# Kernel tables from two small tables of magnitudes, read-outs of the last rows on VectorE, and a new order

## The chip, the cores and the metric

The kernel runs on one core of one Trainium2 chip. A core has five engines with their own instruction queues: PE (TensorE, matrix products; its weight loads are listed as PEld), DVE (VectorE), ACT (ScalarE), POOL (GpSimd) and SP (SyncE, which here issues transfers). All work on an on-chip memory, SBUF, of 128 partitions; matrix products go to PSUM and are copied out ("evicted") by DVE or ACT. Each engine works through its instructions in their order and waits where a semaphore tells it to. The metric is the device time of one execution in microseconds (us), lower is better. Before the change the median of three timed runs is 259.13 us (257.56 to 259.44).

## The reference

The input u is 2048 rows (time) of 512 channels in bf16. Two results are computed from it and mixed by a gate per row.

```python
g = sigmoid((x * gate_w).sum(-1, keepdims=True))
# a: state space model, per channel d with N = 128 complex states n
P = exp(dt[d] * A[d, n] * l)                    # l = 0 .. 2047
K = einsum("dn,dnl,dn->dl", C, P, dt * B).real  # one kernel of 2048 per channel
y = irfft(rfft(u, 4096) * rfft(K, 4096))[:2048] + u * Dskip
# b: linear attention, 32 heads of 16
phi(t) = concat(softmax(t @ w_phi), softmax(-t @ w_phi))
o = phi(q) @ (phi(k).T @ v) / (phi(q) @ phi(k).sum + 1e-6)
out = g * a + (1 - g) * (o @ wo)
```

The exponential of dt * A * l has a magnitude, from the real part of A, and an angle, from the imaginary part. The change concerns the magnitudes.

## The kernel before

**Work and stages.** The preparation builds tables of cosines and sines, the polar form of the state parameters, the spectrum of u (matrix products, evicted as `XAu` and `xst`), and the keys of the attention. At `x_up` (L629) the memory of the preparation is given to the convolution stage. That stage goes through 16 units of 32 channels. For each unit it builds the kernel of the 32 channels over the states as a matrix product of two tables, A (coarse time steps) and R (fine time steps, 64 of them), transforms it (`psA`, `psB`), multiplies it with the spectrum of u (`t`, L1220 and L1223), and goes back (`psz`, `Zr`, transfers `Zd` and `ZT`, `psy`). Between the units lie the queries of the attention (`pq`, `Eq`, `zs`, `ops`). The last units are taken as (12, 13), (14), (15), each with its own way back to the output; here the last four row blocks of each 16 (j = 12 to 15) are read out apart, in what the prediction calls the tail.

**A unit.** Its steps are these:

- `plan_tables` (L992): an argument matrix product (`args`, L1007) from the stored angles `statC` and a selection `selE`, then two sines on ACT, which give cs, 2 x 1024 elements per partition. cs has four buffers.
- `plan_exp` (L1019): an argument matrix product (L1029) from the stored real parts `statE`, an exponential on ACT (E, 1024 elements, through L70), and a product on DVE with the table `Gtab` (El, L1038), 1024 elements: E holds the magnitudes of the 32 upper fine steps, El those of the lower.
- `kgen` (L1075): A1 and A2 (both at L1088) are products of two tables, 2048 elements each, two halves of one tile A. R's upper half is E times cs (L1106), its lower half El times cs (L1110), 2048 elements each. The matrix products `kps` (L178, `kgen_chunk`) multiply A and R: 128 per unit with four terms, or 64 with two, after A's second half has been added to its first on DVE (A3, L1099). `FOURS` holds the choice per unit: 14 units have four terms.
- `kps` is evicted as KD, transformed to `psA`, evicted as XA (L1142 to L1163), and so on.

**The read-outs of the last rows.** `psy` gathers the products of the way back. The attention's part, which is stored in xT, comes in by a matrix product with the identity (L1325, L1337); then DVE multiplies by the gate (`ou`, L1352 to L1361) and the rows go out (L1375). The rows j = 12 to 15 are kept without the gate in Y (in the memory of Ctab, copied by ACT or DVE), added to the attention's last read-out `bps` by an identity product (L958), and multiplied by the gate on ACT (L963) or DVE (L965): `bsg`. Their transfers are L975.

**Order.** All steps are nodes of a `Plan` (L73) with an engine, the nodes they depend on, and the buffers ("rings") that they take and give back. `run` (L146) emits them in the order of `ORDER`, a string of two characters per node; `SIDES` says for each step that can run on either of two engines which one it is, `RINGS` which PSUM ring it takes. The order on each engine is that of the string; nothing is rearranged afterwards. ACT's function tables are loaded (L67) when the next function is of another set than the last one: the exponentials and the sines are of different sets.

Of the kernel before, what the change touches and what calls it, by code (L numbers as in the profile page):

```python
# [72 lines left out]
class Plan:  # L73

    DIGITS = "0123456789abcdefghijklmnopqrstuvwxyzABCDEFGHIJKLMNOPQRSTUVWXYZ-_"
    ORDER = ("0J0K0L0O0N0R0M0f0g0h1b0304050U0i0j0k1c0Y1d0c0d0e0001021x1f111I1o131z0V090a0b0P1g0r0s0t2J0W1A1p1q1B1J1K0-0607081y0Z2x0_0X"
             "0Q2K16171Y1-121Z0D0E0F0l0m0n0x0y0z2B1F1h1_1D1C271G2y102V0A0B0C2X1e182C282W0u0v0w292R2Y2L0o0p0q192D2M2E2P2Q2N2T2O2F0S2a1r"
             "1s1t2H2U2I2d2S0G0H0I2G144u4B1L1u1v1w1E1H2z0T4J4F4C4K151a1R2Z2v4D4N4E4G4L4H4O4R1T2-2_302A1U1V1W4M1M1S4P2e4I51524S4Z1X4Q1O"
             "4V4T4-4W20224_4U1Q2123505h4v4X1i1j1k2w4Y2f55245i4w2h312g5d56534x32542j2i2o5e595758255a5b2l5f5g6_70715j333537341P2p1l1m1n"
             "3638265c5t5u5k1N5l5m5x5y5v4y5n5w5o2k2b2m2c393b3c3d3a3f3e4z2q3g3h3J3j4A3k3i2s3K2r3o3q3r3p5p5q3l3m3n2t2n3L2u3v3x3y3s3t3u3w"  # L80
             "3M7v3C7x3D5r3E3F3z3A3B3N3P3O3R3Q3T3U3S3V3X3W3Z3-3G3H3I3_3Y40737541435z424844494546474a4f4b4c4d4e4h4g4m4o4i4p7u5s724n4j4k"
             "4l4q4r4s5A5B5C5D5E5F5G5H4t7a7w5I7b7476777c7g787_80815J7V7W7X7h7d7H5K7I797e68695L5M7f6a7m7i6b5N7j5O7n7k7y7N7l7o6z5P7z5Q7p"
             "7A5R5S6A5T5U5V7B7E7C8S7q8T7F6c6B6d6e7s7r5W5X5Y6C6f9h9i7D7Y7Z7-7t7J6g7O5Z7G7K7L7M6h8O8Q8U5-5_606D629d61637P9f7Q8P8R8V8Y8Z"
             "8W9e6i6j6k7R6l6m6n9g8_7S6E6o646F90aH7TaI6G6p6q6r6s6H8X7U6I6t65856v956u868d8e6J6K6L8-9196879q926w9r669j93aD9n676M6N6O6PaF"
             "6x8f6y9497988l8m6Q6R6Sb36U6T9kb58n6W9E9F9G886V9H9I9J9o9l9m8t9s6X8u896Y9w9x8a8b8caE6ZaG6-999b9p9a9c9tb2b4dF8gdGaJ8oaN9u82"
             "83849v9y9zaQ8haO9AaR8v9BaK9C9D8i8j8k8p8w9Q9YcAcBcCaLaS9K9L9M9R8xaW9S9ZaXbf8q8r8sbgaMdH9-aPb6dIa4dJa5b7bhaTblacaUdKaVdLbm"
             "eFeGaddMdNaYbcb99TaZ8y8z8AdOb8csba8H9N9O9Pa6cw9U9_a0ct8B8C8Dbb8E8F8GcxbzbAbB8I8Kbd8L8Jbe8Mbibjbk9V9W9XcYcZdPdQdRa-8NcPbt"
             "bubvaecQcVcRa7bna8a_b0boa1a2a3dSdTdUafagcSdVbpdWdXdYb1cWdZa9aaabcubrecbqbsbFbNbwbxbyc-d2edbGcTbOcUcXcybHbIahaiajbJd3akal"
             "ambVc1c_cGcHcIbPd0bWbQc2bRbXd1d4d5bKbLbMeiefbYbCbDbEcvbZd6aqczegc3d7d8d9c4bSbTbUehcDcEcFdaeLdic5eeb-b_c0dbardjejdcekeldk"
             "anaoapc6c7c8cMcNcOeIeJeHcJcKcLeKdddlataudedmavemeMend-d_eoepeNeOePeQdfdgdhasdndodpeqerc9cacbeReSeseTetdqdrdsdtdudveuevew"  # L90
             "awe0cfeUeWeVeXeYe1e-cccdcecgdwche2cidxeZexeyezaAaBaCcje_ckeAeBeCaxayazcpcqcrf0cldye3e4f1cmcncoe6e5e7eDeEdzdAdBdCdDdEf2f3"
             "fdfefff4f5f6e8f7f8f9fafbfce9eafjfkflfgfhfieb")
    SIDES = ("110101010111010000000001010101001010000000100101010010011101110001000000000101000010000000000000000000000000000000000000"
             "1000000001000010101000000001111011010")
    RINGS = ("001011010101010110001000010011000100100100100101100100011000001000000011011110001110100000000000000000100010000000010001"
             "010100110101000000100001001110100100011110000110011011010100011100010110")
    FOURS = ("0111111111111110")
# [72 lines left out]
def kgen_chunk(nc, kps, A, R, four):  # L170

    for e in range(2):
        for g4 in range(4):
            terms = [(k, k) for k in range(2)] if not four else [(0, 0), (2, 0), (1, 1), (3, 1)]
            for i, (ka, kr) in enumerate(terms):
                for dj in range(4):
                    d = 8 * g4 + 4 * e + dj
                    nc.tensor.matmul(kps[32 * dj:32 * dj + 32, g4, e, :], lhsT=A[:, d // 4, 32 * ka:32 * ka + 32, d % 4],  # L178
                                     rhs=R[:, kr, d, :], start=(i == 0), stop=(i == len(terms) - 1), tile_position=(0, 32 * dj), skip_group_check=True)
# [14 lines left out]
def prepare(P, nc, g, evict, psum):  # L194
# [122 lines left out]
    def tiles():  # L317
        F.P, F.Q = (g.ptmp.tile([128, 2, 4, 256], BF16, name=n) for n in ("ppx", "ppy"))
        two = lambda t: [t[:, k].rearrange("p a c -> p (a c)").bitcast(F32) for k in range(2)]
        F.M = g.csp.tile([128, 2, 4, 256], BF16, name="pmag", tag="cs", bufs=4)  # L320
        F.T = two(F.Q) + [g.ptmp.tile([128, 512], F32, name=f"pt{i}")[:] for i in range(3)] + two(F.P) + two(F.M)
        F.xy = F.T[3].bitcast(BF16).rearrange("p (k c) -> p k c", k=2)
        F.B = [g.csp.tile([128, 4, 256], F32, name=f"pb{i}", tag="cs", bufs=4) for i in range(2)]
        F.sc = g.csp.tile([128, 2, 4, 256], BF16, name="trg", tag="cs", bufs=4)
    P.add("X", "x_pt", tiles, take=["cs"] * 4, rw=("", "tmp"))
# [12 lines left out]
    for qi, (k, col) in enumerate((("Are", "dtc"), ("Aim", "dt2"))):  # L338
# [13 lines left out]
        def ds(qi=qi):  # L352
            st = (g.statE, g.statC)[qi]
            for s in range(2):
                for e in range(2):
                    for cc in range(2):
                        r0 = 64 * e + 32 * s + 16 * cc
                        nc.sync.dma_start(out=st[r0:r0 + 16, :, :],
                                          in_=g.pz[qi, s].rearrange("(h c e x) n -> c e x h n", h=8, c=2, e=2)[cc, e])
        P.dma("pzr", 4.0, 2.0, ds, rw=(f"z{qi}", ("stE", "stC")[qi]), move=1.2, cnt=8)  # L360
# [31 lines left out]
    V("p_t", lambda: tt(Tt(2)[:], pA.ps[:, 0], Tt(4)[:], ALU.mult), r="pA t4", w="t2")  # L392
    done(pA, nA, "p_t", lambda: tt(Tt(4)[:], pA.ps[:, 1], Tt(4)[:], ALU.mult), "pA t2", "t4")

    are, aim = (lambda: F.T[2][:]), (lambda: F.T[4][:])
    mag = lambda: F.M[:].rearrange("p k a c -> p (k a c)").rearrange("p (a c) -> p a c", a=4)
    for b in range(8):
        S("p_d", lambda b=b: act(out=g.D[:, 0, b, :], in_=are(), func=ACT.Exp, scale=64.0 * (b - 3.5)), r="t2", w=f"D{b}", tab="L")
    S("p_g", lambda: act(out=g.G[:], in_=are().unsqueeze(2).to_broadcast([128, 512, 2]), func=ACT.Exp, scale=-32.0), r="t2", w="G", tab="L")
    for a in range(4):  # L400
        S("p_ce", lambda a=a: act(out=mag()[:, a, :], in_=are(), func=ACT.Exp, scale=512.0 * a + 255.5), r="t2", w="t7 t8", tab="L")
    F.sg = lambda: g.D[:, 1, :, 256:512].rearrange("p (k a) c -> p k a c", k=2)

    def trig4(name, fill, r, sc, k):
        X, N = (lambda: low(F.B[0][:].rearrange("p a c -> p (a c)").bitcast(I32)).rearrange("p (a c) -> p a c", a=4)), (lambda: F.B[1][:])
# [44 lines left out]
    polar = P.add("X", "x_polar", freed, drop=["cs"] * 4, deps=[n for n in P.nodes if n.name[:2] in ("p_", "st", "pz")])  # L450

    def sel(e):
        g.m32 = g.up.tile([128, 32], BF16, name="m32")
        e.tensor_scalar(out=g.m32[:], in0=g.c128[:, 0:32], scalar1=g.icol["p31"], scalar2=None, op0=ALU.is_equal)
        g.b32 = g.up.tile([128, 32], BF16, name="b32")
        e.tensor_scalar(out=g.b32[:], in0=g.c128[:, 0:32], scalar1=1.0, scalar2=0.5, op0=ALU.mult, op1=ALU.add)
    E("sel0", sel, r="ic", w="sel0", eng="POOL")
    E("sel1", lambda e: e.tensor_tensor(out=g.selE[:], in0=g.m32[:].unsqueeze(2).to_broadcast([128, 32, 32]),
                                        in1=g.b32[:].unsqueeze(1).to_broadcast([128, 32, 32]), op=ALU.mult), r="sel0", w="selE", eng=BOTH)
# [26 lines left out]
    def at3(e):  # L486
        at.gwr = wp.tile([128, 4, 32], BF16, name="gwr")
# [54 lines left out]
def keys_and_spectrum(P, nc, g, psum):  # L542
# [89 lines left out]
    ups = [n for n in P.nodes if n.name not in ("at2", "at3", "wo", "wv", "wsm") and n.name[:2] != "x_"] + [polar]  # L632
    sh = P.add("X", "x_up", shift, ups)

# [6 lines left out]
def attention_keys(P, nc, g, psum, r):  # L641
# [141 lines left out]
    sk = P.add("X", "x_keys", shift_k, [n0, n1, sh] + g.Wqn + kp)  # L783
# [3 lines left out]
def plan_queries(P, nc, g, psum, r):  # L787
# [14 lines left out]
    def block(b, late, yn=()):  # L802
# [38 lines left out]
        def z1():  # L841
            Q.den = g.qp.tile([128, 2, 128], F32, name="den")
            Q.apm = g.qp.tile([128, 2, 128], BF16, name="apm")
# [11 lines left out]
        def z4():  # L855
            nc.vector.tensor_tensor(out=Q.z[:, 0:2, :], in0=Q.z[:, 0:2, :], in1=Q.den[:, 0:1, :].to_broadcast([128, 2, 128]), op=ALU.add)
            Q.den = None

        def z5():
            act(out=Q.apm[:], in_=Q.z[:, 0:2, :], func=ACT.Exp, scale=-1.0)  # L860
# [7 lines left out]
        def aw():  # L868
            nc.sync.dma_start(out=g.apd[b].rearrange("i h m c -> (i h m) c"), in_=Q.apm[:].rearrange("p s t -> p (s t)"))
            Q.apm = None  # L870
# [78 lines left out]
        for ip in range(2 if late else 0):  # L949
# [3 lines left out]
            def pbl(ip=ip, box=box):  # L953
                box.ps = psum([128, 2, 512], "bps")
                for k in range(2):
                    o, i = box.ps[:, k, 0:448], 2 * ip + k
                    out_mm(o, i, slice(0, 448), True)
                    nc.tensor.matmul(o, lhsT=g.ident[:], rhs=g.Y[:, i].rearrange("p q d -> p (q d)")[:, 0:448], start=False, stop=True, skip_group_check=True)  # L958

            def bg(k, j=j, box=box):  # L960
                o, i = xT[:, j + k].rearrange("p k d -> p (k d)")[:, 0:448], box.ps[:, k, 0:448]
                if P.cur.at == "ACT":
                    nc.scalar.activation(out=o, in_=i, func=ACT.Copy, scale=g.gT[:, j + k:j + k + 1])  # L963
                else:
                    nc.vector.tensor_scalar(out=o, in0=i, scalar1=g.gT[:, j + k:j + k + 1], scalar2=None, op0=ALU.mult)  # L965
# [657 lines left out]
```

## Time and profile before

| | us |
|---|---|
| median of three timed runs | 259.13 |
| lowest and highest | 257.56, 259.44 |
| the profiled execution, its own time | 255.31 |
| its span in the profile | 253.4 |
| busy in that span: PE, DVE, ACT, POOL | 196.5, 217.5, 217.8, 8.1 |
| mean granted clock of TensorE | 0.98 |

The span runs from the first to the last instruction of the profiled execution; 1.9 us of its time lie around it. Busy time is the time in which an engine has an instruction under way. In the rows of the profile, L1088 is line 1088 of the kernel, `out<-in` names the tiles, then come partitions x elements and types, a count, the busy time and the mean duration in ns of one, and at the end the idle time of the engine just ahead of these instructions, with what ended it.

### The profile page before, as it was taken

How to read it: one execution, taken by the hardware profiler on the slowest of the kernel's cores; microseconds unless marked ns; L12 is line 12 of the kernel's file. 1: busy time of each engine (PE TensorE's matmuls, PEld its weight loads, DVE VectorE, ACT ScalarE, POOL GpSimd, SP SyncE). 2: the span in 40 equal slices, each digit the busy share in tenths (PEclk: the TensorE clock that was granted, in tenths of full speed). 3: DMA queues.
4: the chain of work that ended last, by engine and by line, in shares of the span. 5: the costliest groups of instructions: out<-in, count | busy, mean ns of one | idle time of the engine just before them, and what ended most of it. 6: DMA issues, size and time to landing. Idle time of an engine off the chain costs nothing.

```text
span 253.4 us, 10143 instructions
## 1 busy us (share of the span) xinstructions
PE 196.5 (78%) x4564; PEld 138.5 (55%) x4564; DVE 217.5 (86%) x299; ACT 217.8 (86%) x266; POOL 8.1 (3%) x19
## 2 busy tenths in 40 slices
PE   0537899999977785987749978788896679989790
PEld 0527555757654671454627756446573557769650
DVE  6879987778999769999999999989989999986531
ACT  4999899998999999989999999999997999773001
POOL 5033000000000000000000000000000000000000
PEclk9999999999999999999986999999999999999997
DMA  5979650000006358906560853169678559999884
GB/s 107 209 142 205 166 152 3 4 3 0 3 0 227 107 189 235 218 3 161 113 172 10 212 126 122 50 213 221 155 227 239 133 156 250 238 221 190 117 151 109
DMA packets 65675, 35.21 MB, mean 139 GB/s; under 512 B 49376, under 2 KB 57184, under 8 KB 65632
## 3 DMA queue, kind: packets, MB, share of 16 engines
q1 hardware_dynamic: 63712, 34.01, 56.0%
q10 hardware_dynamic: 1920, 0.56, 1.0%
q8 instruction: 35, 0.57, 1.0%
q14 instruction: 8, 0.07, 0.1%
HBM read 21.65 MB, written 11.53 MB: 131 GB/s over the span
## 4 chain that ended last, share of the span: by engine, by line
ACT 46%; PE 30%; DVE 7%; issue 6%; DMA 6%; SPq 2%; ACTq 1%; DVEq 0%
ACT cs L70 8%; ACT Eq L70 4%; PE vp L720 4%; PE pk L689 4%; ACT L67 4%; ACT xst L142 3%; ACT XK L142 3%; ACT E L70 3%; PE zk L704 2%; DMA ax<-apd 2%; PE psy L797 2%; ACT XAu L142 2%; DMA ZT<-Zd 2%; ACT KD L142 2%; PE ops L901 2%
## 5 line engine op out<-in xcount | busy, mean ns | idle before, releaser
L1088 DVE TENSOR_TENSOR A<-Ctab,Dtab 128x2048 bf16<-128x2048 bf16 x32 | 38.6, 1221 | 1.5 <-PE kps L178 1.5
L70 ACT ACTIVATE cs<-args 128x1024 bf16<-128x1024 f32 x32 | 31.4, 1068 | 0.5 <-PE args L1007 0.5
L178 PE MATMUL kps<-R,A 128*32 128x64 bf16 x1920 | 21.4, 199 | 5.3 <-DVE A L1088 1.7
L178 PEld LDWEIGHTS <-A 128*32 128x32 bf16 x1920 | 19.1, 116 | 9.8 <-issue 4.4
L1110 DVE TENSOR_TENSOR R<-El,cs 128x2048 bf16<-128x2048 bf16 x16 | 19.5, 1220 | 0.1
L1106 DVE TENSOR_TENSOR R<-E,cs 128x2048 bf16<-128x2048 bf16 x16 | 19.5, 1219 | 0.0
L67 ACT ACT_TABLE_LOAD x14 | 18.0, 1283 | 0.2
L1220 DVE TENSOR_TENSOR t<-XUX,XK 128x2048 bf16<-128x2048 bf16 x14 | 17.0, 1221 | 1.2 <-ACT XK L142 0.7
L70 ACT ACTIVATE E<-args 128x1024 bf16<-128x1024 f32 x16 | 16.7, 1049 | 0.5 <-PE args L1029 0.4
L816 PE MATMUL pq<-xT,Wqp 128*128 128x512 bf16 x64 | 15.1, 379 | 1.9 <-ACT E L70 0.5
L70 ACT ACTIVATE Ek<-pk 128x1024 bf16<-128x1024 f32 x16 | 15.4, 1024 | 0.9 <-PE kvp L738 0.6
L1252 PE MATMUL psz<-t,TI 128*128 128x512 bf16 x60 | 15.5, 380 | 0.5 <-ACT Zr L142 0.3
L70 ACT ACTIVATE Eq<-pq 128x1024 bf16<-128x1024 f32 x16 | 15.6, 1061 | 0.2
L142 ACT CAST XA<-psA 128x1024 bf16<-128x1024 f32 (+1 forms) x15 | 14.2, 989 | 1.8 <-PE psA L185 1.8
L142 ACT CAST XK<-psB 128x1024 bf16<-128x1024 f32 x15 | 15.4, 1060 | 0.1
L720 PE MATMUL vp<-WW,xT 128*128 128x512 bf16 x64 | 15.2, 380 | 0.3 <-ACT Ek L70 0.3
L142 ACT CAST Zr<-psz 128x1024 bf16<-128x1024 f32 x14 | 14.6, 1040 | 0.7 <-PE psz L1252 0.4
L689 PE MATMUL pk<-WW,xT 128*128 128x512 bf16 x64 | 15.0, 380 | 0.0
L185 PE MATMUL psA<-W,KD 128*64 128x128 bf16 x256 | 10.7, 227 | 4.5 <-ACT Zr L142 1.7
L185 PEld LDWEIGHTS <-KD 128*64 128x64 bf16 x256 | 8.5, 113 | 7.9 <-issue 5.4
L191 PE MATMUL psB<-XA,TB 128*128 128x128 bf16 (+2 forms) x192 | 10.0, 201 | 3.2 <-ACT cs L70 1.7
L191 PEld LDWEIGHTS <-TB 128*128 128x128 bf16 x192 | 9.0, 97 | 5.9 <-issue 4.9
(209 smaller groups left out, 473.0 us busy)
## 6 DMA issues: line engine op xcount, KB each, us to landing
XUX<-XUd SPq DMA_DIRECT2D x24, 256.0 KB, 4.6
ax<-apd SPq DMA_DIRECT2D x16, 256.0 KB, 4.5
Zd<-Zr SPq DMA_DIRECT2D x15, 256.0 KB, 4.1
XUd<-xst SPq DMA_DIRECT2D x8, 384.0 KB, 2.9
ZT<-Zd SPq DMA_DIRECT2D x6, 512.0 KB, 6.4
UD<-in_A_u_dram SPq DMA_DIRECT2D x16, 128.0 KB, 4.0
XUX<-XU SPq DMA_DIRECT2D x8, 256.0 KB, 4.5
XU<-xst SPq DMA_DIRECT2D x8, 128.0 KB, 3.2
```

The lines of the kernel that those rows point to most:

```text
L67: return self.nc.scalar.preload_act_table_set(name)
L70: return self.nc.scalar.activation(**kw)
L142: self.nc.scalar.copy(out=o, in_=i)
L178: nc.tensor.matmul(kps[32 * dj:32 * dj + 32, g4, e, :], lhsT=A[:, d // 4, 32 * ka:32 * ka + 32, d % 4], rhs=R[:, kr, d, :], start=(i == 0) ...
L185: nc.tensor.matmul(ps[64 * ri:64 * ri + 64], lhsT=lhsT, rhs=fc.W1[:, ri].rearrange("p r d -> p (r d)"), start=True, stop=True, tile_positi ...
L191: nc.tensor.matmul(ps[:, sl, :], lhsT=fc.TB[:, 3 * (r0 + sl) + 1:3 * (r0 + sl) + 3].rearrange("p a b -> p (a b)"), rhs=XA[:, r0 + sl], sta ...
L689: nc.tensor.matmul(box.ps[:, u, :], lhsT=xT[:, 2 * s2 + u, kt, :], rhs=g.WW[:, kt, :], start=(kt == 0), stop=(kt == 3))
L720: nc.tensor.matmul(box.ps[:, u, :], lhsT=xT[:, 2 * s2 + u, kt, :], rhs=g.WW[:, 4 + kt, :], start=(kt == 0), stop=(kt == 3))
L1088: nc.vector.tensor_tensor(out=c.A[:, :, 64 * k:64 * k + 64, :].rearrange("p q (x b) l -> p x b q l", b=8), in0=cf.unsqueeze(2).to_broadcas ...
L1106: nc.vector.tensor_tensor(out=c.R[:, :, :, 32:64], in0=t.E[:].unsqueeze(1).to_broadcast([128, 2, 32, 32]), in1=t.cs[:], op=ALU.mult)
L1110: nc.vector.tensor_tensor(out=c.R[:, :, :, 0:32], in0=t.L[:].unsqueeze(1).to_broadcast([128, 2, 32, 32]), in1=t.cs[:, ::-1, :, ::-1], op=A ...
L1220: nc.vector.tensor_tensor(out=box.t, in0=Ls[r0 // ns].X[:], in1=box.XK[:].unsqueeze(1).to_broadcast([128, 2, 1024]), op=ALU.mult)
```

## The change

Magnitudes: the 64 fine steps of a unit are written as 8 u + v. In the preparation ACT makes a table E2 (8 values of v, all 512 channels) from the real parts `are`, and after `x_up` a table E1 (8 values of u; that of u = 4 is 1 and is set by POOL). Per unit one DVE product of E1 and E2 gives EL, all 64 magnitudes, 2048 elements, in place of the argument product, the exponential and El. The stored real parts `statE` with their way through memory, and `Gtab`, go. R gets a layout in which four channels lie beside each other; DVE writes runs of four elements, and `kps` reads every fourth. A becomes two half tiles. cs has two buffers in place of four, EL has one; `TJ2` still takes one of the cs buffers late in the stage.

```diff
-        T.E = g.epool.tile([128, 32, 32], BF16, name="E", bufs=g.P.k["E"])
-        box.ps = psum([128, 2, 16, 32], "args")
-        for e in range(2):
-            nc.tensor.matmul(box.ps[:, e], lhsT=g.statE[64 * e:64 * e + 64, h, :], rhs=g.selE[64 * e:64 * e + 64, 16 * cc:16 * cc + 16, :],
-                             start=True, stop=True, tile_position=(64 * e, 0))
...
-        act(out=T.E[:], in_=box.ps[:].rearrange("p e x t -> p (e x) t"), func=ACT.Exp)
...
     def el():
-        T.L = g.epool.tile([128, 32, 32], BF16, name="El", bufs=g.P.k["El"])
-        nc.vector.tensor_tensor(out=T.L[:].rearrange("p c (t k) -> p c t k", k=2), in0=T.E[:].rearrange("p c (t k) -> p c t k", k=2),
-                                in1=g.G[:, 32 * U:32 * U + 32].unsqueeze(2).to_broadcast([128, 32, 16, 2]), op=ALU.mult)
+        T.L = g.epool.tile([128, 2, 32, 32], BF16, name="EL", tag="EL", bufs=1)
+        nc.vector.tensor_tensor(out=T.L[:].rearrange("p e (u v) c -> p (e u) v c", v=8), in0=g.E1[:, :, 32 * U:32 * U + 32].unsqueeze(2).to_broadcast([128, 8, 8, 32]),
+                                in1=g.E2[:, :, 32 * U:32 * U + 32].unsqueeze(1).to_broadcast([128, 8, 8, 32]), op=ALU.mult)
...
+    for v in range(8):
+        S("e2x", lambda v=v: act(out=g.E2[:, v, :], in_=g.are[:], func=ACT.Exp, scale=v + 0.5), r="ar", w=f"E2{v} " + ("t7 t8" if v < 4 else "B0"), tab="L")
...
+    P.add("POOL", "e1m", lambda: nc.gpsimd.memset(g.E1[:, 4, :], 1.0), [sh], rw=("", "E14"))
+    for u in (0, 1, 2, 3, 5, 6, 7):
+        P.add("ACT", "e1x", lambda u=u: g.act(out=g.E1[:, u, :], in_=g.are[:], func=ACT.Exp, scale=8.0 * (u - 4)), [sh], rw=("ar", f"E1{u}"), tab="L")
...
-                c.R = g.rk.tile([128, 2, 32, 64], BF16, name="R")
-                nc.vector.tensor_tensor(out=c.R[:, :, :, 32:64], in0=t.E[:].unsqueeze(1).to_broadcast([128, 2, 32, 32]),
-                                        in1=t.cs[:], op=ALU.mult)
+            def rr(k, c=c, t=t):
+                s = t.cs[:] if k else t.cs[:, ::-1, ::-1]
+                q = lambda x: x.rearrange("p k t (q l) -> p k t q l", l=4)
+                nc.vector.tensor_tensor(out=c.R[:, :, k].rearrange("p q k t l -> p k t q l"), in0=q(t.L[:, k].unsqueeze(1).to_broadcast([128, 2, 32, 32])), in1=q(s), op=ALU.mult)
...
-                                     rhs=R[:, kr, d, :], start=(i == 0), stop=(i == len(terms) - 1), tile_position=(0, 32 * dj), skip_group_check=True)
+                                     rhs=R[:, d // 4, :, kr, :, d % 4], start=(i == 0), stop=(i == len(terms) - 1), tile_position=(0, 32 * dj), skip_group_check=True)
```

Read-outs: Y is multiplied by the gate on DVE as it is copied. `bsg` is one DVE instruction per row block, gate times `bps` plus Y, for all four; the identity products go. In `psy`, too, the identity products go, and DVE adds the stored rows to PSUM ahead of the multiply (`plus`).

```diff
+            def plus(p, y):
+                nc.vector.tensor_tensor(out=p, in0=p, in1=y, op=ALU.add)
...
-                    for d2 in range(2):
-                        nc.tensor.matmul(box.py[:, d2], lhsT=g.ident[:], rhs=bS[:, j0:j0 + nj, off + ng * d2:off + ng * d2 + ng], start=True, stop=False,
-                                         skip_group_check=True)
...
-                    nc.tensor.matmul(o, lhsT=g.ident[:], rhs=g.Y[:, i].rearrange("p q d -> p (q d)")[:, 0:448], start=False, stop=True, skip_group_check=True)
...
-                if P.cur.at == "ACT":
-                    nc.scalar.activation(out=o, in_=i, func=ACT.Copy, scale=g.gT[:, j + k:j + k + 1])
-                else:
-                    nc.vector.tensor_scalar(out=o, in0=i, scalar1=g.gT[:, j + k:j + k + 1], scalar2=None, op0=ALU.mult)
+                nc.vector.scalar_tensor_tensor(out=xT[:, j + k].rearrange("p k d -> p (k d)")[:, 0:448], in0=box.ps[:, k, 0:448], scalar=g.gT[:, j + k:j + k + 1],
+                                               in1=g.Y[:, 2 * ip + k].rearrange("p q d -> p (q d)")[:, 0:448], op0=ALU.mult, op1=ALU.add)
...
+                nc.vector.tensor_tensor(out=g.Y[:, :, Q, do], in0=i, in1=g.gT[:, 12:16].unsqueeze(2).to_broadcast([128, 4, nd]), op=ALU.mult)
```

`ORDER`, `SIDES` and `RINGS` are new strings, and the units' choice changes too: ten units have four terms, and six need A3.

```diff
-    FOURS = ("0111111111111110")
+    FOURS = ("0100111011011110")
```

By the instructions of the two built kernels, the new sides move evictions between DVE and ACT: in the preparation DVE evicts 7 of 16 `XAu` (6 before) and 9 of 16 `xst` (6 before), and both halves of `Wqp` where ACT did; in the convolution stage ACT evicts two more `XA`, one `Zr` and one part of `wo`. `selE` and two small tables are made on DVE where POOL made them. ACT loads its tables 18 times (15 before). Of the transfers of the output ACT issues 10 (8 before) and SP 14 (16 before). On PE, one of the two blocks of `psy` for units 8 to 11 (L797, L799, and its `ZT` products) stands ahead of the last unit's `kps`, where it stood behind it.

More of the change, by code (lines that the diff above doesn't have):

```diff
@@ L1122, in kgen @@
                 g.half = an[1]
-            kps.append(P.add("PE", "kps", kp, an + [rn] + kps, take=([psq, "KD"] if cc == 0 else []), drop=["A", "R"]))
+            kps.append(P.add("PE", "kps", kp, an + [rn] + kps, take=([psq, "KD"] if cc == 0 else []), drop=["A", "A", "R"]))
         def kd(k=None):
@@ L1385, in transform @@
             if two:
-                yn.append(P.add(("ACT", "DVE"), "Y", lambda oy=oy: P.copy(*oy()), (ya or [y]) + [y, o], drop=["psum"]))
+                yn.append(P.add("DVE", "Y", oy, (ya or [y]) + [y, o], drop=["psum"]))
             if end and Q != 0 and (nd > 32 or last):
```

206 lines of the change are left out of this document (100 added, 106 removed).

## The prediction

> **What bounds the kernel now.** I read the busy totals and the chain that ended last, then the windows of three stretches, then the waits of VectorE (DVE) inside the middle one.
>
> ```profile
> span 253.4 us, 10143 instructions
> PE 196.5 (78%) x4564; PEld 138.5 (55%) x4564; DVE 217.5 (86%) x299; ACT 217.8 (86%) x266; POOL 8.1 (3%) x19
> ACT 46%; PE 30%; DVE 7%; issue 6%; DMA 6%; SPq 2%; ACTq 1%; DVEq 0%
> ```
>
> By the totals DVE and ScalarE (ACT) are level, and the chain names ACT. That points at ACT, where the change takes work away. The windows say otherwise. They are cut at the first A product (98.26) and at the end of the last R product (224.67); a fourth lies inside the first. After the length come the busy times of PE, weight loads, DVE, ACT and POOL.
>
> ```profile
> core 0: us, PE busy (x) PEld busy (x) DVE busy (x) ACT busy (x) POOL busy (x), PEclk, DMA share, GB/s
> 0.00:98.26 98.26, 74.67 (x1044) 52.19 (x1044) 81.75 (x151) 90.71 (x118) 8.08 (x19) 1.00 0.45 107
> 30.00:70.00 40.00, 39.65 (x520) 25.33 (x518) 32.79 (x52) 37.50 (x58) 0.00 (x0) 1.00 0.11 30
> 98.26:224.67 126.41, 102.14 (x2930) 71.00 (x2929) 123.02 (x128) 120.27 (x139) 0.00 (x0) 0.97 0.63 163
> 224.67:253.40 28.73, 19.73 (x592) 15.30 (x592) 12.69 (x21) 6.81 (x11) 0.00 (x0) 0.95 0.82 143
> ```
>
> The preparation (98.3 us) leaves DVE idle for 16.5 us, and its heart is full on PE, 39.65 of 40. In the convolution stage DVE is busy 123.0 of 126.4 us: 3.4 us of idle in 126. The tail (28.7 us) is slack on every engine, a chain of short steps. DVE's waits in the middle window:
>
> ```profile
> DVE A L1088 <- PE kps L178: 1.5, 3, 0.6
> DVE t L1220 <- ACT XK L142: 0.7, 1, 0.7
> DVE t L1220 <- issue: 0.3, 1, 0.3
> DVE xT L1352 <- PE psy L1331: 0.2, 1, 0.2
> ```
>
> That is all DVE waits for there. ACT, at 120.3, runs beside it: it is second, and taking from it shortens nothing while DVE is full. So the middle stage is priced by DVE alone.
>
> **The change part by part.** Counts are those of the instructions of the two built kernels; durations are rows of before.
>
> ```profile
> 125.27 0.69 DVE L1038 TENSOR_TENSOR El<-E,Gtab 128x1024 bf16<-128x1024 bf16 x1
> 125.87 1.22 DVE L883 TENSOR_TENSOR Eq<-Eq,ax 128x2048 bf16<-128x2048 bf16 x1
> 127.00 1.22 DVE L1088 TENSOR_TENSOR A<-Ctab,Dtab 128x2048 bf16<-128x2048 bf16 x1
> 128.14 1.22 DVE L1106 TENSOR_TENSOR R<-E,cs 128x2048 bf16<-128x2048 bf16 x1
> ```
>
> Neighbours on DVE overlap a little: from start to start a 2048-element product takes 1.14 us (127.00 to 128.14) and a 1024-element one 0.60 (125.27 to 125.87). These pitches, not the durations, add up.
>
> *The middle stage on DVE.*
>
> ```profile
> L1088 DVE TENSOR_TENSOR A<-Ctab,Dtab 128x2048 bf16<-128x2048 bf16 x32 | 38.6, 1221 | 1.5 <-PE kps L178 1.5
> L1038 DVE TENSOR_TENSOR El<-E,Gtab 128x1024 bf16<-128x1024 bf16 x16 | 11.0, 685 | 0.0
> L1110 DVE TENSOR_TENSOR R<-El,cs 128x2048 bf16<-128x2048 bf16 x16 | 19.5, 1220 | 0.1
> L1099 DVE TENSOR_TENSOR A<-A 128x2048 bf16<-128x2048 bf16 x2 | 2.4, 1222 | 0.0
> L1220 DVE TENSOR_TENSOR t<-XUX,XK 128x2048 bf16<-128x2048 bf16 x14 | 17.0, 1221 | 1.2 <-ACT XK L142 0.7
> ```
>
> - The product EL, 16 of 2048 elements, comes in: 16 x 1.14 = +18.2. The product El, 16 of 1024, goes: 16 x 0.60 = -9.6. The exponential that goes with it stood on ACT, not on DVE.
> - Units with four terms fall from 14 to 10, so the halving sum (L1099) rises from 2 to 6: 4 x 1.14 = +4.6.
> - Four evictions of 1024 elements from PSUM move to ACT (XA twice, Zr, wo), each as long as such a product (1223 ns for xst, below): 4 x 1.14 = -4.6.
> - The R products keep count and size (32) but write runs of four elements. A (L1088) does that already, and takes 1221 ns as the contiguous t (L1220) does: I take 0 (bounds 0 and, if a run of four cost R its speed, a doubling: below).
> - Row multiplies (L1361): one more of 1024 elements here, +1.1.
>
> Sum **+9.8 us**, which nothing covers, since DVE had 3.4 us of idle. That idle I keep: the same PE and ACT edges hold A and t. Bounds: 2 (nearly all of it used up) and 13 (10% idle, were the single EL buffer and the two cs buffers, where four stood, to make DVE wait for ACT).
>
> *What leaves ACT and PE there.*
>
> ```profile
> L70 ACT ACTIVATE E<-args 128x1024 bf16<-128x1024 f32 x16 | 16.7, 1049 | 0.5 <-PE args L1029 0.4
> L70 ACT ACTIVATE Dtab<-pt 128x512 bf16<-128x512 f32 x8 | 4.9, 629 | 0.0
> L178 PE MATMUL kps<-R,A 128*32 128x64 bf16 x1920 | 21.4, 199 | 5.3 <-DVE A L1088 1.7 <-DVE XA L144 1.5 <-issue 1.3
> L178 PEld LDWEIGHTS <-A 128*32 128x32 bf16 x1920 | 19.1, 116 | 9.8 <-issue 4.4 <-DVE A L1088 3.2 <-DVE R L1110 1.2
> L837 PEld LDWEIGHTS <-KVbd 128*32 128x32 bf16 x128 | 3.5, 97 | 0.0
> L1286 PEld LDWEIGHTS <-t 128*32 128x32 bf16 x128 | 2.1, 155 | 0.2
> ```
>
> ACT loses 16 exponentials, 16.7 us by their row, and gains 7 of 512 elements in E1 (7 x 0.63 = 4.4 by Dtab's row), four cs evaluations that no longer fit ahead of the stage and the moved evictions; it ends near 115, below DVE. PE loses 256 of 1920 kps matmuls (256 x 21.4/1920 = 2.9 us) and 32 argument matmuls. Both gains lie beside DVE, so 0. A loss may hide there: kps now reads R at every fourth element (8 bytes). The trace has weights only: 116 ns at 8 bytes, 97 contiguous, 155 at 64. A fifth more on 1664 x 11.1 ns = 18.5 us is 3.7 us, a doubling 18.5; PE has 24 us free, so 0 on the path, unless the last units wait for it.
>
> The Trainium skill, page "Advanced Engine Details and Errata", section "SBUF Cachelines", says that reads hitting a 16-byte line twice run at full rate, so a step of 8 bytes is free. The weight rows here do not bear that out (116 against 97); by the page the read costs 0, by the row 3.7, and the sum is the same either way.
>
> *Preparation.*
>
> ```profile
> L144 DVE CAST xst<-psB 128x1024 bf16<-128x1024 f32 x6 | 7.3, 1223 | 2.2 <-PE psB L596 2.2
> L67 ACT ACT_TABLE_LOAD x14 | 18.0, 1283 | 0.2
> 38.21 1.14 ACT L70 ACTIVATE Dtab<-pt 128x512 bf16<-128x512 f32 x2
> 94.36 3.78 ACT L70 ACTIVATE cs<-args 128x1024 bf16<-128x1024 f32 x4
> 98.16 1.28 ACT L67 ACT_TABLE_LOAD   x1
> ```
>
> DVE gains three xst and one XAu eviction, and of the weight evictions two come and one goes: 5 x 1.14 = +5.7. Small table work, moved from POOL or ACT, adds some 2.2; steps of the state table go (-1.6): +6.3. ACT loses four cs, four evictions of that spectrum and a table exponential (9 x 0.94, by the four cs = -8.5) and 1.8 of other evictions; it gains eight exponentials of E2 (0.51 from start to start, by the pair: 4.1) and three table loads (3.8): -2.4. The ten transfers of the state table E leave SP's queue, which idles there. With 16.5 us of DVE idle, and PE full where it decides, I take **0** (bounds -3, from ACT's relief at 70 to 98 us; +4, where DVE's 6.3 us fall on the late evictions). E1 can start only when the pools change: two cs, a load and seven exponentials, 1.9 + 1.3 + 3.6 = 6.8 us, while DVE has two A products, a sum and the attention's small tables, some 6 us; EL is hardly late.
>
> The Trainium skill, page "ScalarE: Activation LUTs", section "What ACT_TABLE_LOAD costs", adds a drain of about 1.38 us to each load. By it the three loads would be an estimated 8.0 us, not 3.8, and ACT in preparation would gain 1.8 us instead of losing 2.4; with DVE idle as it is, that stays inside the bounds. The trace shows no such gap: cs ends at 98.14 and the load begins at 98.16. I go by the row.
>
> *Tail.*
>
> ```profile
> L958 PE MATMUL bps<-Ctab,ident 128*128 128x448 bf16 x4 | 1.4, 352 | 0.0
> 228.64 1.03 PE L901 MATMUL ops<-Eq,KVbd 128*128 128x256 bf16 x8
> 229.51 0.39 PE L797 MATMUL psy<-wo 128*128 128x128 bf16 x4
> 231.68 0.22 PE L799 MATMUL psy<-diagD,xT 128*128 128x128 bf16 x1
> L1356 DVE TENSOR_TENSOR xT<-psy,gT 128x256 bf16<-128x256 f32 x3 | 1.2, 419 | 0.1
> 247.38 0.63 ACT L963 ACTIVATE xT<-bps,gT 128x448 bf16<-128x448 f32 x1 [2.72 <-DMA out_dram<-xT]
> 248.05 0.68 DVE L965 TENSOR_SCALAR xT<-bps,gT 128x448 bf16<-128x448 f32 x1 [2.63 <-ACT xT L963]
> 250.09 0.92 SPq L975 DMA_DIRECT2D out_dram<-xT  x2
> ```
>
> The attention block of 2.4 us (229.51 to 231.90) is now issued ahead of the last kps, out of the tail: about -2.4; the ops of 1.0 stay or move with it. Identity matmuls go, 1.4 in the read-outs and a like amount in psy, off a chain that PE holds only in part: I count -1.4. The 2.6 us in which DVE waited for ACT's last read-out, which stood behind ACT's own transfer issues, goes when DVE does all four: -2.6. Against it DVE takes six additions (five at 0.34, one at 0.60), two more read-outs (2 x 0.60) and three more gate products (1.2), 4.7 us, of which the serial half, 2.3, counts. What is late next is the issue of the last transfers: each of SP's pairs takes 0.92 (250.09) to 2.7, and the end stays some 2.4 us behind the last, so I add 0.9. Sum -2.4 - 1.4 - 2.6 + 2.3 + 0.9 = **-3.2** (bounds 0: the block's ZT transfer, which is queued on PE ahead of the last kps, gives it all back; -7: the serial DVE work costs nothing and ops moves).
>
> *Sum.* 0 + 9.8 - 3.2 = +6.6 us, a span of 260.0. The profiled execution took 255.31, 1.9 beyond its span, and would take 261.9. The timed median is 259.13, 3.8 above that execution, so I put the 6.6 on the median: **265.7 us**, +2.5%.
>
> **The rivals.** *DVE stalls.* With one EL, two cs and half tiles of A, DVE could idle 10% of the stage, 13 us for 3.4: +9.6, so 275. For it: cs needs ACT in time, ACT holds other work in order, and once TJ2 has taken its cs buffer (late in the stage) one is left, so a unit's cs starts only after the R products of the unit before. Against: between those R products and the next DVE has five or more products, 5.7 us, for 1.9 us of cs; the waits above show only 2.7 us, and ACT gets lighter. In its worst form R's runs of four cost DVE its rate, 32 x 1.14 = +36, 302 us; the row of A speaks against that.
>
> *No change within 1%.* The tail gives 7 and the idle of the stage falls from 3.4 to 2: 9.8 - 1.4 - 7 = +1.4, 260.5. For it: the tail's slack on every engine. Against: the issue of transfers stays.
>
> *Faster.* The preparation packs: the new order lets DVE fill the 16.5 us of idle there. With none left the first A comes at 98.3 - 16.5 + 6.3 = 88.1, and the kernel takes 265.7 - 10.2 = 255.5. To be faster by over 1% the first A must come by 89.1 (9.2 earlier, of which 6.6 pay the rest). For it: DVE and ACT both have slack there, and the evictions are spread anew. Against: PE is full from 30 to 70, and the loads of the input set the start.
>
> That the change doesn't do what it says, that the exponentials stay, is excluded by the instructions.
>
> **How the numbers follow.** Forecast 0.62 (+1 to +4.5%); stalls 0.13, of which 0.02 is the slow R; within 1% 0.16; faster 0.09. A measurement of this kernel tells about 1% from no change. The range, 258 to 274, reaches from the no-change case to the stalls: below it lie the faster case and a little of the no-change one (0.12), above it somewhat over half of the stalls (0.08).
>
> **What would show it.** DVE busy near 133 in the stage between the first A and the last R, with 3 us idle, would show the main term right; EL at 1.22 us with 16 rows; R at 1.22. First A near 98. From the last R to the end about 25.5. Wrong it would be if DVE's stage ran under 128 us, if the first A came by 90, or if R or kps took over a fifth longer than before.

## The result and the profile after

The changed kernel takes 266.79 us (median of 4 runs, 263.79 to 268.39), the kernel before 258.35 us beside it: a ratio of 1.0353, 95% interval 1.0280 to 1.0426. A second comparison, made along with the experiments, gave 266.45 against 258.36, ratio 1.0252 (1.0147 to 1.0356). It is slower, by some 8 us (8.4 and 8.1 by the medians, 9.1 and 6.5 by the ratios); the forecast was 6.6 us and 265.7. Some executions were disturbed: the medians below are over all executions of a kernel, the ratios and their intervals leave the disturbed ones out.

The profiled execution takes 266.83 us with a span of 265.0, 11.6 more than before (253.4). That is more than the 8 us between the medians, because the profiled execution of before was a quick one, 255.31 against a median of 258.35. The first lines are the page's span, busy totals and chain; the windows are cut as in the prediction, at the first A product and at the end of the last R product (columns: length, then busy time of PE, weight loads, DVE, ACT, POOL, then the granted clock of PE, the share and the rate of the transfers).

```profile
span 265.0 us, 9537 instructions
PE 198.8 (75%) x4247; PEld 143.8 (54%) x4264; DVE 236.1 (89%) x316; ACT 211.4 (80%) x263; POOL 5.3 (2%) x15
DVE 19%; PE 19%; ACT 17%; issue 6%; DMA 3%; SPq 2%; DVEq 0%; ACTq 0%
```
```profile
0.00:98.26 98.26, 75.35 (x1039) 53.08 (x1047) 86.43 (x160) 90.46 (x118) 5.32 (x15) 0.97 0.47 102
98.26:240.45 142.19, 107.19 (x2675) 78.28 (x2683) 132.91 (x128) 116.60 (x137) 0.00 (x0) 0.90 0.58 147
240.45:265.00 24.55, 16.25 (x539) 12.45 (x540) 16.75 (x28) 4.34 (x9) 0.00 (x0) 0.98 0.84 155
```

The preparation is as long as before, to the hundredth: 98.26. The convolution stage grew from 126.41 to 142.19, **+15.8**, and the tail shrank from 28.73 to 24.55, **-4.2**. DVE is busy 132.9 us in the stage, as forecast (133). Its idle time there is 9.3 us, though, where 3.4 was kept. The waits of DVE in the stage, and the groups behind them:

```profile
DVE A L1076 <- PE kps L177: 4.2, 5, 1.2
DVE t L1212 <- ACT XK L141: 2.1, 1, 2.1
DVE Eq L889 <- DMA ax<-apd: 1.8, 3, 0.9
DVE EL L1028 <- ACT E L70: 0.6, 1, 0.6
```
```profile
L177 PE MATMUL kps<-R,A 128*32 128x64 bf16 x1664 | 29.5, 243 | 8.1 <-ACT XA L141 2.4 <-DVE A L1087 2.3 <-DVE A L1076 1.2
L1096 DVE TENSOR_TENSOR R<-EL,cs 128x2048 bf16<-128x2048 bf16 x32 | 38.9, 1220 | 0.3
L1028 DVE TENSOR_TENSOR EL<-E,E 128x2048 bf16<-128x2048 bf16 x16 | 19.5, 1218 | 0.6 <-ACT E L70 0.6
L1087 DVE TENSOR_TENSOR A<-A 128x2048 bf16<-128x2048 bf16 x6 | 7.3, 1221 | 0.1
```

EL and R take what they were said to take (1218 and 1220 ns). What was not foreseen is kps: 256 matmuls fewer, and yet 29.5 us in place of 21.4; one takes 17.7 ns of PE (29.5 / 1664), before 11.1. The product that writes the next A waits for it, 4.2 us against 1.5.

### The profile page after: what moved, and what is told of

Read it like the earlier page. It is cut to its first block, busy times and chain, and to the rows that moved or that the text cites. A ratio compares the mean times of both kernels' runs of the same rounds, so it can differ in the third digit from the quotient of the medians.

```text
span 265.0 us, 9537 instructions
## 1 busy us (share of the span) xinstructions
PE 198.8 (75%) x4247; PEld 143.8 (54%) x4264; DVE 236.1 (89%) x316; ACT 211.4 (80%) x263; POOL 5.3 (2%) x15
## 4 chain that ended last, share of the span: by engine, by line
DVE 19%; PE 19%; ACT 17%; issue 6%; DMA 3%; SPq 2%; DVEq 0%; ACTq 0%
PE kps L177 6%; DVE R L1096 4%; ACT cs L70 4%; DVE A L1076 3%; DMA ax<-apd 3%; ACT XA L141 2%; ACT Eq L70 2%; DVE t L1212 2%; ACT Zr L141 2%; PE psy L804 2%; PE psz L1244 2%; ACT E L70 2%; ACT L67 2%; PE psB L190 2%; PE ops L907 1%
## 5 line engine op out<-in xcount | busy, mean ns | idle before, releaser
L1096 DVE TENSOR_TENSOR R<-EL,cs 128x2048 bf16<-128x2048 bf16 x32 | 38.9, 1220 | 0.3
L177 PE MATMUL kps<-R,A 128*32 128x64 bf16 x1664 | 29.5, 243 | 8.1 <-ACT XA L141 2.4
L177 PEld LDWEIGHTS <-A 128*32 128x32 bf16 x1664 | 26.6, 119 | 11.8 <-issue 5.1
L141 ACT CAST XA<-psA 128x1024 bf16<-128x1024 f32 (+1 forms) x17 | 15.9, 979 | 6.1 <-PE psA L184 6.1
L1028 DVE TENSOR_TENSOR EL<-E,E 128x2048 bf16<-128x2048 bf16 x16 | 19.5, 1218 | 0.6 <-ACT E L70 0.6
L141 ACT CAST XK<-psB 128x1024 bf16<-128x1024 f32 (+1 forms) x17 | 16.1, 990 | 4.6 <-PE psB L190 4.4
L1212 DVE TENSOR_TENSOR t<-XUX,XK 128x2048 bf16<-128x2048 bf16 x14 | 17.1, 1220 | 2.2 <-ACT XK L141 2.1
L141 ACT CAST KD<-kps 128x1024 bf16<-128x1024 f32 (+2 forms) x10 | 8.4, 846 | 10.3 <-PE kps L177 10.3
L184 PE MATMUL psA<-W,KD 128*64 128x128 bf16 x256 | 10.0, 227 | 7.1 <-ACT KD L141 4.5
L70 ACT ACTIVATE Eq<-pq 128x1024 bf16<-128x1024 f32 x16 | 15.0, 1026 | 0.0
```

Source lines behind the costliest of these rows:

```text
L70: return self.nc.scalar.activation(**kw)
L141: self.nc.scalar.copy(out=o, in_=i)
L184: nc.tensor.matmul(ps[64 * ri:64 * ri + 64], lhsT=lhsT, rhs=fc.W1[:, ri].rearrange("p r d -> p (r d)"), start=True, stop=True, tile_positi ...
L1028: nc.vector.tensor_tensor(out=T.L[:].rearrange("p e (u v) c -> p (e u) v c", v=8), in0=g.E1[:, :, 32 * U:32 * U + 32].unsqueeze(2).to_broa ...
L1096: nc.vector.tensor_tensor(out=c.R[:, :, k].rearrange("p q k t l -> p k t q l"), in0=q(t.L[:, k].unsqueeze(1).to_broadcast([128, 2, 32, 32] ...
L1212: nc.vector.tensor_tensor(out=box.t, in0=Ls[r0 // ns].X[:], in1=box.XK[:].unsqueeze(1).to_broadcast([128, 2, 1024]), op=ALU.mult)
```

## The experiments

Three questions are open: whether VectorE's sum is what sets the stage, what the slow kps costs, and whether the tail shrank for the reasons given. The edits were made in the changed kernel and in the kernel before, so that the same cost is seen in both orders.

**VectorE's sum in the order of before.** Each El is issued twice.

```diff
-        nc.vector.tensor_tensor(out=T.L[:]...
+        for _ in range(2):
+            nc.vector.tensor_tensor(out=T.L[:]...
```

> The kernel before, with each product El issued twice in a row, 16 x 0.60 = 9.6 us more on VectorE and nothing else. Theory 1 and theory 3 expect 7 to 9.6 us more than before, since VectorE had 3.4 us of idle in the stage: 266 to 268. Theory 4 expects that VectorE's sum matters little: under 3 us more.

Measured: 265.88 us, ratio 1.0305 (1.0258 to 1.0351). The stage, in the window view:

```profile
98.26:234.34 136.08, 107.50 (x2904) 73.46 (x2914) 133.78 (x144) 120.64 (x138) 0.00 (x0) 0.90 0.58 152
```

VectorE was given 9.6 us more by the prediction's pitch (its busy time rose by 10.8); the stage became 9.7 us longer (126.41 to 136.08) and the kernel 8.2 us slower. So in the order of before, VectorE sets the stage one for one, with 2.3 us of idle. The prediction's main argument is shown there, for an addition of the size that the change makes. The granted clock of the stage fell to 0.90, as in the changed kernel, and VectorE did not wait more for it.

**VectorE's sum in the changed kernel.** EL covers its first half, and both R products read that.

```diff
-                nc.vector.tensor_tensor(... in0=q(t.L[:, k].unsqueeze(1)...
+                nc.vector.tensor_tensor(... in0=q(t.L[:, 0].unsqueeze(1)...
-        ... T.L[:] ... in0=g.E1[:, :, ...] ... to_broadcast([128, 8, 8, 32])
+        ... T.L[:, 0] ... in0=g.E1[:, 0:4, ...] ... to_broadcast([128, 4, 8, 32])
```

The unedited kernel was run beside it.

> The changed kernel, unedited, so that the others have it beside them on the same chip. Theory 1 (VectorE's own work sets the time of the convolution stage: 132.9 us busy of 142.2) and theory 2 (the extra idle of VectorE there, 9.3 us against 3.4, comes from slower kps matmuls, 17.7 ns each against 11.1, which hold the half tiles of A) both expect 264 to 268 us and the first A near 98.

> The product EL covers its first half alone (1024 elements) and both R products read that half, so half of the magnitudes are left out. Theory 1 expects 16 x (1.14 - 0.60) = 8.6 us less, so 258 us. If VectorE were not what sets the stage, its idle would grow by as much and the time would fall by under 3 us.

Measured: 266.45 us for the unedited (ratio to before 1.0252), 266.1 us with half of EL (1.0278, 1.0195 to 1.0361). The stage of the unedited and of the half, from the windows of their profiles, and then two waits of DVE in the stage of the half:

```profile
96.47:239.97 143.50, 106.95 (x2682) 77.61 (x2682) 132.88 (x128) 116.78 (x137) 0.00 (x0) 0.90 0.60 145
```
```profile
97.57:236.37 138.80, 104.34 (x2682) 76.99 (x2682) 125.02 (x128) 116.53 (x137) 0.00 (x0) 0.94 0.60 150
DVE A L1076 <- PE kps L177: 5.7, 6, 1.8
DVE Eq L889 <- DMA ax<-apd: 4.6, 4, 1.8
```

VectorE lost 7.9 us of work; its stage lost 4.7 us in the profiled execution (the fastest of its four), and over the executions the kernel lost nothing that can be told. DVE's idle rose from 10.6 to 13.8: it waits a little more for XK (0.7 to 1.9), for kps (4.7 to 5.7) and for the attention's transfer ax (4.0 to 4.6). So theory 1 alone falls for the changed kernel: with less work VectorE is not what sets the stage there.

**The step of kps.** kps reads 64 neighbours in place of every fourth element, and in the other kernel the reverse.

```diff
-     rhs=R[:, d // 4, :, kr, :, d % 4], start=...
+     rhs=R[:].rearrange("p q k r t l -> p (q k r t l)")[:, (32 * kr + d) * 64:(32 * kr + d) * 64 + 64], start=...
```

> Only the moving operand of kps is changed: 64 elements beside each other in place of every fourth, so it multiplies other elements of R and the output is not the reference's. Theory 2 expects kps back near 11 ns each (about 11 us of PE less), A's wait for kps down from 4.2 us to about 1.5, VectorE's idle in the stage near 4 us and the time 4 to 6 us shorter. Theory 1 alone expects kps shorter beside VectorE and the time within 1 us. If 17.7 ns comes from the granted clock (0.90 in the stage) and not from the step of 8 bytes, kps stays above 15 ns here.

> The kernel before, with kps reading every fourth element of R in place of neighbours, so it multiplies other elements. If the step of 8 bytes is what slows the matmul, kps goes from 11.1 to about 17.5 ns each (12 us more on PE). Theory 1 expects this beside VectorE: within 2 us of before. Theory 3 expects 2 to 6 us more, since PE is then on the second limit. If the granted clock was the cause, kps stays near 11 ns.

Measured: 264.89 us for the changed kernel without the step, -1.6 by the medians, but by the ratio (1.0256, 1.0186 to 1.0326) the same as the unedited 1.0252; 262.16 us for the kernel before with it (1.0150, 1.0093 to 1.0208), +4.4 by the medians and +3.9 by the ratio. First the group of kps, the stage and DVE's first wait in the kernel before with the step, then kps, the stage and DVE's waits in the changed kernel without it:

```profile
L178 PE MATMUL kps<-R,A 128*32 128x64 bf16 x1920 | 34.3, 243 | 3.0 <-DVE A L1088 1.2
98.25:228.82 130.57, 114.06 (x2911) 81.76 (x2921) 123.45 (x128) 120.36 (x138) 0.00 (x0) 0.96 0.59 157
DVE A L1088 <- PE kps L178: 4.3, 5, 1.5
```
```profile
L177 PE MATMUL kps<-R,A 128*32 128x64 bf16 x1664 | 20.2, 210 | 10.4 <-DVE A L1087 3.6
96.73:239.12 142.39, 101.19 (x2682) 71.47 (x2682) 132.43 (x128) 117.03 (x137) 0.00 (x0) 0.87 0.57 145
DVE t L1212 <- ACT XK L141: 5.5, 2, 4.4
DVE Eq L889 <- DMA ax<-apd: 2.3, 2, 1.3
DVE A L1076 <- PE kps L177: 1.1, 1, 1.1
```

That the step slows kps is shown: 243 ns and 17.9 ns of PE each, at a granted clock of 0.96 as at 0.90, and 12.1 without the step in the changed kernel. In the order of before it costs 4.2 us of stage by itself, and A's wait for kps grows from 1.5 to 4.3. In the changed kernel its removal takes most of A's wait away (4.2 to 1.1), as theory 2 said, but neither the time nor the stage gets shorter (142.39 against 142.19 and 143.50): DVE now waits for XK, and its idle is 10.0. So the slow kps alone is not what the extra idle hangs on, and theory 2 falls as the account of the time. Theory 1 expected the unchanged time here, but it fell with the half of EL.

**Both at once.** The two edits to the changed kernel together; and in the kernel before, the doubled El and the step together.

> Both edits in one, kps reading 64 neighbouring elements and EL of 1024 elements, so half of the magnitudes are left out and other elements of R are multiplied. Each alone gained under 2 us by the medians. Theory 3 (two limits lie side by side in the stage, VectorE's sum and the path kps, KD, psA, XA, psB, XK through PE and ACT, so that shortening one finds the other) expects 7 to 9 us less than the changed kernel, 257 to 259. Theory 4 (neither sets the stage; the new order of the instructions with its waits for the transfer ax and for ACT does) expects 262 us or more.

> The kernel with both edits to the changed one again, for a profile at a granted clock like the others': EL of 1024 elements and kps reading neighbours, so half of the magnitudes are left out and other elements multiplied. Theory 3 (two limits side by side) expects a stage of about 142 - 8.6 - 1 to 4, so 130 to 133 us, and 257 to 260. Theory 4 (the order's own waits) expects a stage above 136 us and 262 or more.

> The kernel before with both of the costs that were put in one at a time: El issued twice (its stage was 136.1 us) and kps reading every fourth element (130.6 us; 126.4 without either), so other elements are multiplied. Theory 5 (the two costs of the change add up, and explain its stage of 142.2 us without the order) expects 126.4 + 9.7 + 4.2 = 140 us for the stage and 269 to 271 by the median. Theory 6 (the slow kps hides beside the longer VectorE, and what the changed kernel loses beyond VectorE's sum comes from its order) expects 136 to 138 and 265 to 267.

The first kernel was run twice, ten executions in all. Two take 257.23 and 260.10 us at a mean granted clock of 0.945 and 0.927, seven take 262.4 to 266.6 us at 0.911 to 0.922 (one lies far off, at 295); the medians are 264.95 and 264.66. The profile of the 257.23 us execution:

```profile
96.59:231.25 134.66, 97.84 (x2694) 69.74 (x2694) 124.74 (x128) 116.54 (x137) 0.00 (x0) 0.91 0.61 155
DVE Eq L889 <- DMA ax<-apd: 3.8, 3, 1.6
DVE t L1212 <- ACT XK L141: 2.1, 3, 1.1
DVE A L1076 <- PE kps L177: 1.6, 3, 1.1
```

There the stage is 134.7 us, 8.8 less than the unedited 143.5 and above the 130 to 133 expected, at the same clock in the stage (0.91 and 0.90). VectorE's work fell by 8.1 and its idle is still 9.9 us, now at ax and XK. Two limits side by side (theory 3) fit the time of that execution, the idle that stays at ax and at ACT's XK fits theory 4; most executions do not get there, and neither theory is excluded. The kernel before with both costs took 266.76 us, ratio 1.0347 (1.0256 to 1.0438). With the doubled El alone it was 265.88 (1.0305): on top of VectorE's 9.6 us the step adds about 1 us, which is in the range of theory 6. The profiled execution (375 us) is far off, so the stage of this kernel is not known. That the changed kernel's stage, 6.1 us above 136.1, owes what lies beyond VectorE's sum to its own order and buffers follows by elimination: no run changed the order or the number of buffers alone.

**The choice of four terms.** `FOURS` is one string in each kernel.

```diff
-    FOURS = ("0100111011011110")
+    FOURS = ("0111111111111110")
```
```diff
-    FOURS = ("0111111111111110")
+    FOURS = ("1111111111111111")
```

> The choice of four terms as before the change (14 units of 16), so the sum A3 runs 2 times in place of 6 and kps has 1920 matmuls in place of 1664. Theory 1 expects 4 x 1.14 = 4.6 us less. Theory 2 expects that 256 more kps at 17.7 ns (4.5 us on PE), and A's halves held longer in four more units, give it back: within 2 us of the changed kernel.

> The kernel before with four terms in all 16 units: two sums A3 go from VectorE (2 x 1.14 = 2.3 us) and 128 matmuls kps come (1.4 us on PE). By theory 1 the stage shrinks by 2.3 us, to 124, and the median to 255.5. If A3 rather frees the tile for the next unit early, as four terms in the changed kernel were slower, the time is the same or up to 2 us more.

Measured: the changed kernel with 14 units of four terms 270.24 us, ratio 1.0460 (1.0373 to 1.0548), 3.8 us by the medians and 5 us by the ratios *slower* than with 10; the kernel before with 16 such units 274.7 us, ratio 1.0560 (1.0468 to 1.0652). Neither was expected. The stage of the first, and DVE's first wait in it:

```profile
97.72:243.80 146.08, 111.85 (x2939) 82.13 (x2938) 128.79 (x124) 117.06 (x137) 0.00 (x0) 0.89 0.57 142
DVE A L1076 <- PE kps L177: 13.2, 9, 4.8
```

VectorE is 4.1 us less busy, near the 4.6 of four sums of 1.14, and waits 13.2 us for A in place of 4.2. There are two half tiles of A. The sum A3 releases one of them and halves the matmuls that hold the other; without it the next unit's A waits. For the kernel before the loss, 12 us in its fastest execution (270.4), is more than this explains; its profiled execution (279.8 us, at a granted clock of 0.83) is far off the others, and the cause stays open.

**The tail.** The read-outs of the change alone, in the kernel before; and in the changed kernel, the identity products in psy in place of VectorE's additions.

```diff
-                    nc.tensor.matmul(o, lhsT=g.ident[:], rhs=g.Y[:, i]...
-                if P.cur.at == "ACT":
-                    nc.scalar.activation(out=o, in_=i, func=ACT.Copy, scale=g.gT[:, j + k:j + k + 1])
...
+                nc.vector.scalar_tensor_tensor(out=o, in0=i, scalar=g.gT[:, j + k:j + k + 1], in1=g.Y[:, 2 * ip + k]..., op0=ALU.mult, op1=ALU.add)
```

> The kernel before with the read-outs of the last rows as in the change: Y multiplied by the gate on VectorE, all four bsg on VectorE with Y added, no identity product there (psy keeps its own). The prediction's terms give -2.6 for the wait for ACT's last read-out, about -0.7 for the identity products and +0.6 for VectorE's part: 2.5 to 3 us less than before, 255.5. The rival, that the issue of the last transfers sets the end, expects under 1 us less.

> The changed kernel with the identity products back in psy and without VectorE's six additions to PSUM. The prediction's terms (2.3 us of serial work on VectorE in the tail, against identity products of about 1.4 on PE) expect the tail 0 to 1 us shorter than 24.6 to 25.4. The rival, that PE is what the tail's chain runs on, expects it 1 to 2 us longer.

Measured: the read-outs alone 258.19 us, ratio 1.0053 (1.0004 to 1.0103), no gain; the identity products back 267.27 us, ratio 1.0368 (1.0280 to 1.0457), no difference from the changed kernel that can be told. VectorE's last line in the kernel before with the new read-outs, the same in the changed kernel, and the tail of the changed kernel with identity products:

```profile
250.82 1.27 DVE L962 SCALAR_TENSOR_TENSOR xT<-bps,gT,Ctab 128x448 bf16<-128x448 f32 x2 [2.63 <-PE bps L958]
```
```profile
258.72 1.86 DVE L969 SCALAR_TENSOR_TENSOR xT<-bps,gT,Ctab 128x448 bf16<-128x448 f32 x3
```
```profile
243.19:268.40 25.21, 17.09 (x548) 13.01 (x548) 14.26 (x23) 4.34 (x9) 0.00 (x0) 0.94 0.82 153
```

In the order of before, VectorE waits 2.63 us for PE's `bps` where it had waited 2.63 us for ACT's read-out: another wait took its place (in this execution the tail ran at a granted clock of 0.86, 0.95 before). In the changed kernel's own order the last three read-outs follow each other with no wait ahead of them, so there that wait is gone. The additions cost the tail nothing that can be seen (25.2 us, in an execution 1% above that kernel's median, against 24.6 and 25.4). No kernel of this study beats the one before.

## Why the prediction was right or wrong

The time (265.7 forecast, 266.8 and 266.5 measured) and the direction were right, and so was the view that DVE, not ACT, prices the stage, in the order of before. That the time came so close is in part luck, as the sum below the list shows. Step by step:

- *Preparation, 0:* right. The first A comes at 98.26 in both profiles, though DVE is busy 4.7 us more there. In five other profiles of the changed kernel and its edits it comes at 96.5 to 97.7, up to 1.8 us earlier, within the bounds.
- *The middle stage's DVE sum, +9.8:* right in size, 123.0 to 132.9 us busy, that is +9.9. That such a sum lengthens the stage one for one is shown by the doubled El.
- *"That idle I keep":* wrong, and the largest error. The reason given was that the same PE and ACT edges hold A and t. They do, but they are later: the waits at A went from 1.5 to 4.2 and at XK from 0.7 to 2.1, and the transfer ax (1.8) came in. The idle went from 3.4 to 9.3 us, towards the bound of 13 that the prediction gave. The runs show it is not one stall: take kps's step away and XK is late, halve EL and kps and ax are late.
- *kps's read at every fourth element, "0 on the path":* the size failed. It was priced from the weight rows at a fifth, 3.7 us; it costs 60%, 11 us of PE (29.5 against 1664 x 11.1 ns = 18.5), between that and the doubling that the prediction also named. The reason for the 0, that PE has 24 us free, does not hold in general: in the order of before the step alone costs 4.2 us of stage. In the changed kernel the 0 is borne out by the time, since taking the step away gains nothing, though A waits for kps there.
- *A3, +4.6:* the term stands in VectorE's busy time, but as a cost it has the wrong sign: with four sums fewer, and the order as it is, the changed kernel is 4 to 5 us slower. The work that a sum saves elsewhere, matmuls and the time that A is held, was left out.
- *Tail, -3.2:* measured -4.2 in the profiled pair. The tail of before is not always 28.7: it took 29.0 and 31.5 us in two edits that leave it alone, while the changed kernel and its edits show 24.2 to 25.4 (the execution of 295 us aside), so the gain may be larger. Which terms it consists of is open. The -2.6 for ACT's last read-out is not gained by the new read-outs alone, though in the changed kernel's order the wait is gone; for the -1.4 of identity products, those in psy make no difference that can be seen. The attention's block issued ahead of the last kps, and the rest of the new order, no run moved alone.
- *EL hardly late:* right, 0.6 us.

So the sum 0 + 9.8 - 3.2 was 0 + 15.8 - 4.2: an error of 6.0 in the stage and one of 1.0 in the tail that went the other way. In the profiled pair the kernel is 11.6 us slower, not 6.6. By the medians it is 8, and that the forecast of 265.7 lies so near is luck to that extent: the error of 6.0 in the stage is in part hidden by a median of before that lies 3 us above its profile. The stall rival, put at 0.13 for 275 us, was in part what happened, beside the forecast and not instead of it. Of the causes it names, the half tiles of A show in the waits (4.2); the single EL cost 0.6, and no wait of DVE for cs shows.

The prediction has no term for the granted clock. Windows of two us inside the changed kernel's stage show it at one half after PE had little to do; the first two lines are PE's timeline there, then come the windows, and the last line is a window of the kernel before:

```profile
126.48 1.19 PE L177 MATMUL kps<-R,A 128*32 128x64 bf16 x64 [2.39 <-ACT XA L141]
132.91 1.20 PE L177 MATMUL kps<-R,A 128*32 128x64 bf16 x64 [2.29 <-DVE A L1087]
```
```profile
128.00:130.00 2.00, 1.49 (x7) 0.86 (x6) 1.74 (x2) 1.99 (x4) 0.00 (x0) 0.50 0.98 222
130.00:132.00 2.00, 0.61 (x2) 0.10 (x1) 1.51 (x2) 2.00 (x3) 0.00 (x0) 0.50 0.13 42
132.00:134.00 2.00, 1.09 (x68) 1.09 (x72) 2.00 (x3) 1.98 (x2) 0.00 (x0) 0.50 0.34 94
138.00:140.00 2.00, 1.04 (x32) 0.97 (x33) 2.00 (x5) 1.32 (x3) 0.00 (x0) 1.00 0.03 9
```
```profile
134.00:136.00 2.00, 1.96 (x20) 1.10 (x19) 1.96 (x4) 1.94 (x3) 0.00 (x0) 0.50 0.00 0
```

The Trainium skill, page "TensorE: Matmul & The Clock Gate", sections "What's actually happening" and "HAM oscillation — how this bites in real kernels", says that PE runs at half clock after an idle window of about 3.4 us, and at full clock after a busy one. The trace agrees with the two levels, 0.50 and 1.00 in these rows. It does not show an idle stretch of 3.4 us ahead of them: PE waits 2.39 us before 126.48, and the half clock begins within two us after that. Over the stage the clock is 0.90 against 0.97 before. A PE that is kept waiting then returns its results later, which could make ACT and VectorE wait again. This might account for gains that vanish, since the two quick executions of the combined edit had a higher clock than the seven others. But no run held the clock fixed, and three things speak against it as the whole account: the kernel before has a stretch at half clock too; with the doubled El its stage ran at 0.90 with only 2.3 us of idle on VectorE; and the changed kernel's own executions show no such link (263.79 us at a mean clock of 0.949, 268.39 at 0.945). It is argued, not shown.

## What to carry to other kernels

When the busiest engine has 3 us of idle in 126, an added 10 us costs 10: that estimate held. But removing that much work from the changed kernel again did not give the time back (7.9 us of VectorE for nothing that can be told), because other waits took its place. So price what the new order and the new buffers (two half tiles of A, one EL, two cs) make late, and not only the busy sums; which of them did it here is open. An operation that adds work to the bound engine and frees a buffer early may be worth its price: try the choice before costing it.

## What the runs showed of the hardware

A matmul of 64 columns whose moving operand in bf16 is read at every fourth element takes 17.7 to 17.9 ns of PE in a stream of four column groups, against 11.1 for neighbours (12.1 in the changed kernel, at a clock of 0.87): 60% more in the kernel before, where the weight rows at the same step show 20% (116 against 97 ns). The Trainium skill, page "Advanced Engine Details and Errata", section "SBUF Cachelines", read as the prediction reads it, would have it free, with two hits per line of 16 bytes; the measurement decides, and it is not. The time with the step barely depends on the granted clock: 128 matmuls take 2.18 us at 0.50 and 2.22 us at 1.00, while without the step they take 1.90 at half clock and 1.27 at full. The first two rows are of the changed kernel, from two of its executions, the others of the one without the step:

```profile
143.35 2.18 PE L177 MATMUL kps<-R,A 128*32 128x64 bf16 x128 [1.18 <-ACT XK L141]
157.07 2.22 PE L177 MATMUL kps<-R,A 128*32 128x64 bf16 x128 [1.12 <-ACT cs L70]
```
```profile
142.90 1.90 PE L177 MATMUL kps<-R,A 128*32 128x64 bf16 x128 [0.56 <-ACT XK L141]
156.12 1.27 PE L177 MATMUL kps<-R,A 128*32 128x64 bf16 x128 [1.16 <-ACT cs L70]
```

VectorE's products keep their speed where they write runs of four elements (R) or read two operands that are each repeated along one dimension (EL): 1220 and 1218 ns for 2048 elements, against 1220 for the contiguous t.
